# An issue order written out for the first 14 steps of an attention and FFN kernel

## Chip, core and metric

The kernel runs on one core of a Trainium2 chip. The metric is the device time of one execution in microseconds; lower is better. TensorE (PE) multiplies, VectorE (DVE) and ScalarE (ACT) work on tiles, GpSimd (POOL) helps, and SyncE (SP) issues the DMAs.

## What is computed

Attention of two kinds is added per head, and an FFN with a squared ReLU follows. All inputs are float32 (q, k, v and `w_in` eight times as large as drawn); the weights arrive as 8-byte words and are split in the kernel.

```python
B, H, S, D = q.shape                      # 8, 8, 576, 64; factor = 4, scale = 1/8
q_d, k_d, v_d = means over 4 neighbouring positions        # 144 positions
out_up = repeat(softmax(scale * q_d @ k_d.T) @ v_d, 4)
mask = abs(pos[:, None] - pos[None, :]) < 4
out_local = softmax(where(mask, scale * q @ k.T, -1e9)) @ v
x = (out_up + out_local)  ->  4608 tokens x 512
h = maximum(x @ w_in, 0)                  # 512 x 2048
out = (s * h * h + b) @ w_out             # 2048 x 512
```

## The kernel before

**FFN.** The tokens are cut into 18 blocks `t` of 256, the 2048 hidden columns into 8 pairs `p` of 256. A step (t, p) is `gemm1` (24 matmuls into one bank `ph`: high part times high, high times low, low times high), then on ScalarE ReLU, square and the rounding to `gh`, on VectorE the rest `gl`, then `gemm2` (12 matmuls into the two banks of `po` that collect block t). `gemm2` stands two or three steps behind. The order of steps is (0,0), (1,0), (0,1), (1,1) and so on to (1,6): steps 0 to 13; then block 2 with pairs 0 to 6: steps 14 to 20; then pair 7 of blocks 0 to 2; then blocks 3 to 17.

**Weights.** Pair p of `w_in` and `w_out` is loaded as 64-bit words into a stage buffer (`load_w`, `wst`) and split by `convert` into a float32 value `f`, its rounded part `hi` and the rest `lo`: one ScalarE multiply, four VectorE instructions on `es`, one ScalarE cast, one VectorE subtraction. A conversion here means one such run over 512 columns; a pair of weights has four. Pair 7 comes in eight quarters through buffers `pv` (`load_quarter`). `add_rows` adds up the rows of `w_out` on VectorE into `bias`, 31 additions of 512 columns, and `column_sums` makes b times their sum of it, used by the outputs.

**Attention.** A batch has four pairs of heads. For batches 0 to 2 `first_unit` does a pair: `down` (q and k summed by four into `qd` and `kd`, scores `sa`, exponentials `pd`, transposes `tp` and `tr`, product `up`) and the banded part (scores `sl`, `pl`, transpose, block matrix `db`, product `ol`), added into `x`. The pairs of batch 0 have rooms of their own in the buffers of later weights (`make_room`, zeroed by `clear`). `split_x` makes `xh` and `xl` from x for a block of tokens. A block needs all four pairs of its batch; block 2 needs batches 0 and 1.

**What sets the order.** The program is written as a sequence, and a scheduler lays out each engine's instructions by priorities and its own costs; each engine then runs its own list in order. Batch 0 has a high priority (offset 400), the conversions other ones (`BEHIND`), batch 1 is spread over the first steps (`advance`, `target`). A tile's bank in PSUM is fixed by its tag (`bank(i, ...)`).

Of the kernel before, what the change touches and what calls it, by code (L numbers as in the profile page):

```python
# [56 lines left out]
W_MAX = (1.875 - 2.0 ** -23) * 2.0 ** (31 - 127)  # L57

# [4 lines left out]
def attention_ffn_kernel(ctx, tc, qk, vw_in, vr_in, vdm, qkn, vn, w_in, w_out, s_in, b_in, out):  # L63
# [40 lines left out]
    def load_pair(b, hp):  # L104
        if (b, hp) in ld:
            return
        own = {}
        if b == 0 and hp:
            room[hp] = make_room(hp)
            own = room[hp]["load"]  # L110

        def load(tag, shape, src, pool=one):
            t = own[tag] if tag in own else pool.tile(shape, F32, tag=tag, name="t" + tag)
            nc.sync.dma_start(t, src)
            return t

        tqk = load("qk", [P, 2, SP], qk[b, hp], two)
        tvr = load("vr", [P, FAC, D], vr_in[b, hp])
        tvd = load("vd", [KM, FAC, P], vdm[b, hp])
        tvw = load("vw", [P, NG, P], vw_in[HP * b + hp]) if HP * b + hp < EU else None  # L120
        ld[(b, hp)] = (tqk, tvw, tvr, tvd)

    load_pair(0, 0)
# [4 lines left out]
    load_pair(0, 1)  # L128
# [43 lines left out]
    nc.vector.memset(db, 0.0)  # L174
# [7 lines left out]

    def clear(i):
# [30 lines left out]
    def convert(st, hi, lo, op, p):  # L214


        n = hi.shape[1]
        top, low = st[:, :, 1], st[:, :, 0]
        if p in (0, 1, 7):
            f = two.tile([P, n], F32, tag="pv", name="es")  # L220
        else:
            f = one.tile([P, n], F32, tag="xl2" if op == "i" else "os", name="es")
        w = f.bitcast(I32)


        nc.scalar.mul(f, top.bitcast(F32), 2.0 ** -112)
        nc.vector.tensor_scalar(f, f, W_MAX, -W_MAX, ALU.min, ALU.max)
        nc.vector.tensor_scalar(w, w, 3, 0x7FFFFFF8, ALU.logical_shift_left, ALU.bitwise_and)
        nc.vector.scalar_tensor_tensor(w, low, 29, w, ALU.logical_shift_right, ALU.bitwise_or)
        nc.vector.scalar_tensor_tensor(w, top, -0x80000000, w, ALU.bitwise_and, ALU.bitwise_or)  # L230
        nc.scalar.copy(hi, f)
        for i in range(0, n, 512):
            js = slice(i, min(i + 512, n))
            nc.vector.tensor_tensor(lo[:, js], f[:, js], hi.bitcast(F32)[:, js], ALU.subtract)

    def split_w(p):
        with tc.high_priority(offset=-BEHIND.get(p, 0)):
            split_parts(p)

    def split_parts(p):  # L240
        wi[p] = one.tile([P, 2, NK, 256], F32R, tag=f"wi{p}", name="wi")
        wo[p] = one.tile([P, 2, 2, DM], F32R, tag=f"wo{p}", name="wo")
        for op, w in (("i", wi[p]), ("o", wo[p])):
            fl = w.rearrange("p s k f -> p s (k f)")
            if p < len(STAGE):
                st = wst.pop((p, op))
                for j in range(0, 1024, CHUNK[p]):
                    js = slice(j, j + CHUNK[p])
                    convert(st[:, js], fl[:, 0, js], fl[:, 1, js], op, p)
            else:  # L250
                for i in range(4):
                    cs = slice(256 * i, 256 * i + 256)
                    convert(load_quarter(p, op, i), fl[:, 0, cs], fl[:, 1, cs], op, p)
# [14 lines left out]
    def down(b, hp, banks, tmp, dg):  # L268

        _, qc, vdr, vm = dg  # L270
        tqk, _, tvr, tvd = ld[(b, hp)]
        qt, kt = tqk[:, 0], tqk[:, 1]

        qd = tmp([P, SD], "qd")
        kd = tmp([P, SD], "kd")
        nc.vector.tensor_reduce(
            qd, qt[:, 0:S].rearrange("p (s j) -> p s j", j=FAC), AX.X, ALU.add)
        nc.vector.tensor_reduce(
            kd, kt[:, 3 : 3 + S].rearrange("p (s j) -> p s j", j=FAC), AX.X, ALU.add)
        for h in range(2):  # L280
            hs = slice(64 * h, 64 * h + 64)
            nc.scalar.copy(
                qc[hs, :, GQ * h : GQ * h + GQ], qd[hs].rearrange("p (i s) -> p i s", i=NQ))
# [17 lines left out]
        with first(b):  # L301
            for i in range(NQ):
                nc.tensor.matmul(sa[:, i], qc[:, i], kd, start=True, stop=True)  # L303
        nc.vector.tensor_reduce(dmx[:, 0], sa, AX.X, ALU.max, negate=True)
        nc.scalar.mul(dmx[:, 1], dmx[:, 0], SCALE / 16)
# [38 lines left out]
    def first_unit(b, hp, banks):  # L344
# [20 lines left out]
        tqk, vw, _, _ = ld[(b, hp)]  # L365
# [3 lines left out]
        dn = down(b, hp, banks, tmp, dg)  # L369
        next(dn)  # L370
        yield
        next(dn)
        yield

        own = room[hp] if b == 0 and hp else None
        pl = own["pl"] if own else two.tile([P, 2 * NG, 32], F32, tag="pl", name="pl")
        sm = own["sm"] if own else two.tile([P, 2, 2 * NG], F32, tag="sm", name="sm")
        lmx, lsm = sm[:, 0], sm[:, 1]  # L380
        for h in range(2):
            sl = banks([P, NG, 32], "sl")
            nc.tensor.matmul(sl, idb, maskb, start=True, stop=False)
            hs = slice(64 * h, 64 * h + 64)
            for g in range(NG):
                for w in range(4):
                    c0 = TW * (4 * g + w)
                    nc.tensor.matmul(
                        sl[32 * w : 32 * w + 32, g, :],
                        qt[hs, c0 : c0 + 32], kt[hs, c0 : c0 + 32],  # L390
                        start=False, stop=g == NG - 1, tile_position=(64 * h, 32 * w))
            hg = slice(h * NG, h * NG + NG)
            nc.vector.tensor_reduce(lmx[:, hg], sl, AX.X, ALU.max)
            nc.vector.tensor_tensor(
                pl[:, hg], sl, lmx[:, hg].unsqueeze(2).to_broadcast([P, NG, 32]), ALU.subtract)
            yield
        nc.scalar.activation(pl, pl, AF.Exp, scale=SCALE)
        nc.vector.tensor_reduce(lsm, pl, AX.X, ALU.add)
        nc.vector.tensor_scalar(lsm, lsm, 1e-9, None, ALU.add)
        nc.vector.reciprocal(lsm, lsm)  # L400
        (nc.vector if b else nc.gpsimd).tensor_tensor(
            pl, pl, lsm.unsqueeze(2).to_broadcast([P, 2 * NG, 32]), ALU.mult)
        yield
        next(dn)
        yield
        next(dn)
        if own:
            pt = take(sc, spots["vt"], [P, 2 * NG, 32])
        else:
            pt = two.tile([P, 2 * NG, 32], F32, tag="pl", name="pt")  # L410
        nc.vector.transpose(pt, pl)
        for w in range(4):
            ws = slice(32 * w, 32 * w + 32)
            nc.scalar.copy(bd[ws, :, ws], pt[ws])
        yield
# [4 lines left out]
        ups = tmp([P, SD], "ups")  # L420
        nc.scalar.copy(ups, up)
        yield
        for f in range(2):
            n = S // 2 // FAC
            ol = banks([P, S // 2], "ol")
            for gg in range(NG // 2):
                g = f * (NG // 2) + gg
                for h in range(2):
                    hs = slice(64 * h, 64 * h + 64)
                    pw = bd[:, h * NG + g, :].rearrange("p (w c) -> p w c", w=4)  # L430
                    nc.tensor.matmul(  # L431
                        ol[hs, 96 * gg : 96 * gg + 96], vw[:, g, hs], pw[:, :, 0:TW],
                        start=True, stop=True)
            nc.vector.tensor_tensor(
                x[:, hp, f * (S // 2) : (f + 1) * (S // 2)].rearrange("p (s j) -> p s j", j=FAC),
                ol.rearrange("p (s j) -> p s j", j=FAC),
# [333 lines left out]
```

## Time and profile before

| | |
|---|---|
| time of the runs | 970.22 us median of 3 (969.37 to 974.18) |
| span of the profiled execution | 970.7 us (its own time is not told apart from the runs) |
| TensorE busy | 938.7 us, 97% |
| VectorE, ScalarE, GpSimd busy | 637.7, 475.0, 418.0 us |
| granted TensorE clock, mean | 1.000 |
| moved by DMA | 86.26 MB |

Busy time counts an instruction from start to end, and instructions of one engine overlap a little. An engine's idle time is what its busy time leaves of a stretch. In the tables of windows each engine has its busy microseconds and its count of instructions; in the timeline a row gives start, length, engine, line, instruction and, in brackets, the idle time just before it and what ended that.

### The profile page before, as it was taken

Reading aid. Unit: us, or ns where it says so; the run is one execution under the profiler, and the core shown is the slowest. Engines: PE = TensorE matmul, PEld = TensorE weight load, DVE = VectorE, ACT = ScalarE, POOL = GpSimd, SP = SyncE. Lnnn points to the kernel's source line nnn. Section 1 sums busy time; section 2 is a strip of 40 time slices with the busy share of each in tenths; the row PEclk is TensorE's granted clock in tenths of the full one; section 3 lists DMA queues with packets and bytes.
Section 4 is the critical chain, followed back from the end, with each engine's and each line's share of the span. In section 5 each row is a group of like instructions: output and inputs, shape, how many; then the busy total and the mean of one; then the engine's idle time right before and its main releaser. Section 6 shows DMA issues by size and latency. Waiting matters only on the chain.

```text
span 970.7 us, 18541 instructions
## 1 busy us (share of the span) xinstructions
PE 938.7 (97%) x7316; PEld 843.4 (87%) x7316; DVE 637.7 (66%) x1175; ACT 475.0 (49%) x1141; POOL 418.0 (43%) x455
## 2 busy tenths in 40 slices
PE   5769999999999999999999999999999999999998
PEld 4559988888999999998888899989899999998987
DVE  5999996864567878787787878787878521211121
ACT  5878775553754453545363545453635433333231
POOL 9421011101066686776868786867676200000000
PEclk9999999999999999999999999999999999999999
DMA  9736512112243232323241424242412000000000
GB/s 316 261 121 210 172 60 78 49 42 73 101 134 113 77 110 72 102 70 133 67 136 66 135 68 131 72 134 69 136 55 76 1 22 1 23 1 22 1 23 22
DMA packets 32103, 86.26 MB, mean 89 GB/s; under 512 B 3344, under 2 KB 7952, under 8 KB 32016
## 3 DMA queue, kind: packets, MB, share of 16 engines
q1 hardware_dynamic: 32016, 85.08, 26.6%
q8 instruction: 57, 0.93, 0.4%
q14 instruction: 30, 0.25, 0.1%
HBM read 75.63 MB, written 9.44 MB: 88 GB/s over the span
## 4 chain that ended last, share of the span: by engine, by line
PE 74%; DVE 9%; DMA 8%; POOL 5%; ACT 2%; issue 2%; SPq 0%; DVEq 0%; ACTq 0%; POOLq 0%
PE ph L556 11%; PE ph L557 11%; PE ph L558 11%; PE po L603 11%; PE po L601 11%; PE po L602 11%; DMA tqk<-in_qk_dram 3%; POOL pr L466 3%; POOL acc L488 3%; DMA wst<-in_moe_w_out_dram 2%; PE sa L303 2%; DVE bias L579 1%; PE up L339 1%; PE ol L431 1%; DMA lqk<-in_qkn_dram 1%
## 5 line engine op out<-in xcount | busy, mean ns | idle before, releaser
L556 PE MATMUL ph<-xh,wi 128*128 128x256 f32 x1152 | 325.4, 283 | 3.7 <-ACT xh L542 2.5
L557 PE MATMUL ph<-xl,wi 128*128 128x256 f32 x1152 | 323.9, 281 | 0.0
L558 PE MATMUL ph<-xh,wi 128*128 128x256 f32 x1152 | 323.6, 281 | 0.0
L466 POOL TENSOR_TENSOR pr<-lqk 128x576 f32<-128x576 f32 x140 | 201.2, 1461 | 73.2 <-DMA lqk<-in_qkn_dram 29.2
L556 PEld LDWEIGHTS ph<-xh,wi 128*128 128x128 f32 x1152 | 217.5, 189 | 11.2 <-ACT xh L542 2.8
L557 PEld LDWEIGHTS ph<-xl,wi 128*128 128x128 f32 x1152 | 217.4, 189 | 5.4 <-issue 0.2
L558 PEld LDWEIGHTS ph<-xh,wi 128*128 128x128 f32 x1152 | 217.6, 189 | 0.3
L566 ACT ACTIVATE ph<-ph 128x512 f32<-128x512 f32 x144 | 83.8, 582 | 229.0 <-PE ph L558 223.2
L601 PE MATMUL po<-wo,gh 128*128 128x512 f32 x456 | 180.7, 396 | 0.0
L602 PE MATMUL po<-wo,gh 128*128 128x512 f32 x456 | 180.5, 396 | 0.0
L603 PE MATMUL po<-wo,gl 128*128 128x512 f32 x456 | 177.9, 397 | 0.0
L569 DVE TENSOR_TENSOR gl<-ph,gh 128x512 fp32r<-128x512 f32 x114 | 77.8, 683 | 115.8 <-ACT gh L568 115.5
L488 POOL TENSOR_TENSOR acc<-acc,pv 128x576 f32<-128x576 f32 x80 | 114.4, 1430 | 57.1 <-DVE acc L488 29.5
L468 DVE TENSOR_REDUCE st<-pr 128x9 f32<-128x576 f32 x140 | 105.9, 757 | 37.7 <-POOL pr L466 35.4
L292 POOL TENSOR_TENSOR dq<-vq 64x64 f32<-64x64 f32 x58 | 22.8, 393 | 197.4 <-PE up L337 195.3
L603 PEld LDWEIGHTS po<-wo,gl 128*128 128x128 f32 x456 | 85.7, 188 | 17.6 <-issue 0.2
L487 DVE TENSOR_TENSOR pv<-lv,st 128x576 f32<-128x576 f32 x120 | 87.5, 747 | 18.8 <-POOL acc L488 18.4
L601 PEld LDWEIGHTS po<-wo,gh 128*128 128x128 f32 x456 | 85.7, 188 | 15.9 <-ACT gh L568 0.6
L602 PEld LDWEIGHTS po<-wo,gh 128*128 128x128 f32 x456 | 85.7, 188 | 15.8
L568 ACT CAST gh<-ph 128x512 fp32r<-128x512 f32 x114 | 66.9, 587 | 64.3 <-PE po L602 62.4
L567 ACT ACTIVATE ph<-ph 128x512 f32<-128x512 f32 x144 | 83.7, 582 | 3.2
L602 PE MATMUL po<-wo,gb 128*128 128x512 f32 x120 | 47.1, 392 | 0.0
(149 smaller groups left out, 1239.3 us busy)
## 6 DMA issues: line engine op xcount, KB each, us to landing
tqk<-in_qk_dram SPq DMA_DIRECT2D x30, 584.0 KB, 4.1
lqk<-in_qkn_dram SPq DMA_DIRECT2D x20, 768.0 KB, 4.2
lv<-in_vn_dram SPq DMA_DIRECT2D x20, 480.0 KB, 3.4
out_dram<-os SPq DMA_DIRECT2D x17, 512.0 KB, 3.1
wst<-in_moe_w_in_dram SPq DMA_DIRECT2D x7, 1024.0 KB, 6.5
wst<-in_moe_w_out_dram SPq DMA_DIRECT2D x7, 1024.0 KB, 5.3
tvd<-in_vdm_dram SPq DMA_DIRECT2D x29, 160.0 KB, 2.9
tvr<-in_vr_dram SPq DMA_DIRECT2D x29, 128.0 KB, 3.1
```

Of the source, the lines that this page charges most:

```text
L466: nc.gpsimd.tensor_tensor(pr, lqk[:, 0:CH], lqk[:, CH + o : 2 * CH + o], ALU.mult)
L468: nc.vector.tensor_reduce(ls[:, :, o], pr, AX.X, ALU.add)
L487: nc.vector.tensor_tensor(pv, lv[:, o : o + CH], w, ALU.mult)
L488: (nc.vector if o % 3 == 1 else nc.gpsimd).tensor_tensor(acc[:, :, h], acc[:, :, h], pv, ALU.add)
L556: nc.tensor.matmul(ph[:, j], wi[p][:, 0, k, f], xh[:, k], start=(k == 0), stop=False)
L557: nc.tensor.matmul(ph[:, j], wi[p][:, 0, k, f], xl[:, k], start=False, stop=False)
L558: nc.tensor.matmul(ph[:, j], wi[p][:, 1, k, f], xh[:, k], start=False, stop=(k == NK - 1))
L566: nc.scalar.activation(ph, ph, AF.Relu)
L567: nc.scalar.activation(ph, ph, AF.Square)
L601: nc.tensor.matmul(po[m], gh[:, j, ms], wo[p][:, 0, j], start=first, stop=False)
L602: nc.tensor.matmul(po[m], gh[:, j, ms], wo[p][:, 1, j], start=False, stop=False)
L603: nc.tensor.matmul(po[m], gl[:, j, ms], wo[p][:, 0, j], start=False, stop=last)
```

## The change

The steps of batches 0 and 1, of the conversions of pairs 0 to 6 and of the first FFN steps become generators that stop after each piece of work on one engine (`banded` in place of `first_unit`'s body, `products1`, `upper`, `lower`, `products2`, `begin_x`, `third_x`). A string `PLAN` of 447 words names whose turn it is: `d0` to `d7` are the `down` parts of the eight pairs, `l0` to `l7` the banded parts, `v` the sums of values, `c0` to `c27` the conversions, `x` and `y` the splitting of x, `G`, `R`, `V`, `H` a half of the first product, the ScalarE part, `gl` and a half of the second product. `in_order` chains the instructions of each of four engines in the order in which they were issued, so the scheduler keeps that order among them; others may still go between. After the plan the old loop goes on from step 14.

Besides: the query blocks of batch 0 are loaded first; `clear` writes zeros on ScalarE and VectorE in place of GpSimd; the first two weight pairs are staged in different buffers; every `f` lies in `pv` (before, four tags were used); batch 1's chains each have one PSUM bank; the offsets' mask is made later; `add_rows` begins with pair 0 in place of 7, and is called from step 14 on; pair 7 is converted from step 14 on (before, step 11).

```diff
-STAGE = (6, 6, 7, 6, 7, 6, 7)
-CONVERT_AT = (1, 2, 4, 6, 7, 8, 11)
-CHUNK = (512, 512, 512, 1024, 1024, 512, 1024)
-BEHIND = {1: 400, 2: 100, 4: 100, 5: 400}
+STAGE = (7, 6, 7, 6, 7, 6, 7)
+CHUNK = 512
+PLAN = (
+    "d0 l0 d0 d1 d0 l0 d1 d2 l1 d0 l0 d2 d3 d0 v0 d1 l0 d0 d3 d0 l0 d2 d1 d0 l1 d1 d2 l1 l0 "
...
     def clear(i):
-        for j in range(0, n + QV, 488):
-            nc.gpsimd.memset(da[:, j : min(j + 488, n + QV)], 0.0)
-        nc.gpsimd.memset(vm, 0.0)
+        for part in (da[:, n : n + QV], vm, da[:, 0:n]):
+            if i == 3:
+                nc.vector.memset(part, 0.0)
+            else:
+                nc.scalar.copy(part, zero.to_broadcast([P, part.shape[1]]))
...
-        if p in (0, 1, 7):
-            f = two.tile([P, n], F32, tag="pv", name="es")
-        else:
-            f = one.tile([P, n], F32, tag="xl2" if op == "i" else "os", name="es")
+        f = two.tile([P, n], F32, tag="pv", name="es")
...
     def add_rows(p):
-        if p == NFP - 1:
+        if p == 0:
             nc.vector.tensor_tensor(bias, parts.pop(), parts.pop(), ALU.add)
...
+    @contextlib.contextmanager
+    def in_order():
+        traced = nc.cur_bb.bb.instructions
+        last = traced[-1]
+        yield
+        start = next(k for k in reversed(range(len(traced))) if traced[k] is last) + 1
+        for i in traced[start:]:
+            if i.engine in ENGINES:
+                if i.engine in tail:
+                    tc.add_manual_dep(i, tail[i.engine].name, ...)
+                tail[i.engine] = i
...
+    at = {"sa": 5, "tp": 5, "up": 5, "tr": 6, "sl0": 6, "sl1": 5, "ol": 6}
+    bk = {0: banks(*range(8)), 1: lambda shape, name: bank(at[name], shape, name)}
...
+    with tc.high_priority(offset=400):
+        with in_order():
+            for name in plan:
+                next(streams[name], None)
...
+    begin = 2 * HF
+    for st in range(begin, len(order)):
...
+        if st == begin:
+            split_w(NFP - 1)
+        if st - begin < NFP:
+            add_rows(st - begin)
```

What this does to the order of instructions is seen best on two engines. First VectorE at the start of the FFN, before: `es` are the steps of conversions, `xl` the rest of x, `x<-ol` the attention's sum of a pair.

```order
L543 TENSOR_TENSOR xl<-x,xh 128x1024
L227 TENSOR_SCALAR es<-es 128x512
L434 TENSOR_TENSOR x<-ol,ups 128x288
L234 TENSOR_TENSOR wi<-es,wi 128x512
L434 TENSOR_TENSOR x<-ol,ups 128x288
L234 TENSOR_TENSOR wo<-es,wo 128x512
L228 TENSOR_SCALAR es<-es 128x512
L227 TENSOR_SCALAR es<-es 128x512
L229 SCALAR_TENSOR_TENSOR es<-wst,es 128x512
```

The same place after, around the first `gl`, L642; L248 to L252 are the four steps on `es`.

```order
L251 SCALAR_TENSOR_TENSOR es<-wst,es 128x512
L252 SCALAR_TENSOR_TENSOR es<-wst,es 128x512
L642 TENSOR_TENSOR gl<-ph,gh 128x512
L248 TENSOR_SCALAR es<-es 128x512
L658 TENSOR_TENSOR bias<-bias,wo 128x512
L249 TENSOR_SCALAR es<-es 128x512
L251 SCALAR_TENSOR_TENSOR es<-wst,es 128x512
L252 SCALAR_TENSOR_TENSOR es<-wst,es 128x512
L258 TENSOR_TENSOR wo<-es,wo 128x512
L658 TENSOR_TENSOR bias<-bias,wo 128x512
```

Additions to `bias`, which before begin after `gl` of step 14, now stand among the first steps, and steps that read each other's result stand next to each other.

Then TensorE at the end of batch 0, before: `sl`, `tp`, `up` of batch 1's first pair stand ahead of the first matmul of the FFN, L556.

```order
L383 MATMUL sl<-maskb,idb 128x192
L388 MATMUL sl<-tqk 32x32 x24
L337 MATMUL up<-flat 128x144
L339 MATMUL up<-flat 128x144 x2
L322 MATMUL tp<-ident,pd 80x96
L325 MATMUL tp<-ident,pd 80x96 x2
L327 MATMUL tr<-ident,pd 64x96 x3
L337 MATMUL up<-ptr,dq 128x144
L339 MATMUL up<-ptm,dq 128x144 x2
L431 MATMUL ol<-flat 64x96 x12
L556 MATMUL ph<-xh,wi 128x256
```

After, with the FFN's matmuls at L622:

```order
L469 MATMUL ol<-flat 64x96 x12
L373 MATMUL up<-flat 128x144
L375 MATMUL up<-flat 128x144 x2
L469 MATMUL ol<-flat 64x96 x12
L426 LDWEIGHTS idb
L426 MATMUL sl_813<-maskb,idb 128x192
L431 MATMUL sl_813<-tqk 32x32 x24
L622 MATMUL ph<-xh,wi 128x256
```

Of batch 1 only one block of scores is left ahead of the FFN; the rest of its first pair comes after it.

More of the change, by code (lines that the diff above doesn't have):

```diff
@@ L102, in make_room, with load_parts, load_pair @@
                 "sm": take(pl, at + 384, [P, 2, 2 * NG])}
[L104 to L108, printed above, removed]
-            room[hp] = make_room(hp)
-            own = room[hp]["load"]
-        def load(tag, shape, src, pool=one):
+    def load_parts(b, hp, parts):
+        if b == 0 and hp and hp not in room:
+            room[hp] = make_room(hp)
+        own = room[hp]["load"] if b == 0 and hp else {}
+        got = ld.setdefault((b, hp), {})
+        for tag in parts:
+            shape, src, pool = {
+                "qk": ([P, 2, SP], qk[b, hp], two),
+                "vr": ([P, FAC, D], vr_in[b, hp], one),
+                "vd": ([KM, FAC, P], vdm[b, hp], one),
+                "vw": ([P, NG, P], vw_in[min(HP * b + hp, EU - 1)], one)}[tag]
             t = own[tag] if tag in own else pool.tile(shape, F32, tag=tag, name="t" + tag)
             nc.sync.dma_start(t, src)
[L115 to L123, printed above, removed]
+            got[tag] = t
+    def load_pair(b, hp):
+        if (b, hp) not in ld:
+            load_parts(b, hp, ("qk", "vr", "vd") + (("vw",) if HP * b + hp < EU else ()))
+    for hp in range(HP):
+        load_parts(0, hp, ("qk",))
+    for hp in range(HP):
+        load_parts(0, hp, ("vr", "vd"))
+    load_parts(0, 0, ("vw",))
     ident = cst.tile([P, P], F32, name="ident")
     make_identity(nc, ident)
-    load_pair(0, 1)
     mask = cst.tile([P, 3, 32], F32, name="mask")
@@ L236, in split_w @@
     def split_w(p):
-        with tc.high_priority(offset=-BEHIND.get(p, 0)):
-            split_parts(p)
+        for chunk in split_parts(p):
+            for _ in chunk:
+                pass
     def split_parts(p):
@@ L266, in first, with add_values @@
         return tc.high_priority() if b >= 3 else contextlib.nullcontext()
[L268 to L283, printed above, removed]
+    def add_values(b, hp, tmp, dg):
+        _, _, vdr, vm = dg
+        tvr, tvd = ld[(b, hp)]["vr"], ld[(b, hp)]["vd"]
         vt = tmp([P, 2, P], "vt")
@@ L292, in down @@
             ve.tensor_tensor(vdr[hs, hs], vq[hs, 0], vq[hs, 1], ALU.add)
+    def down(b, hp, banks, tmp, dg):
+        _, qc, vdr, vm = dg
+        tqk = ld[(b, hp)]["qk"]
+        qt, kt = tqk[:, 0], tqk[:, 1]
+        qd = tmp([P, SD], "qd")
+        kd = tmp([P, SD], "kd")
+        nc.vector.tensor_reduce(
+            qd, qt[:, 0:S].rearrange("p (s j) -> p s j", j=FAC), AX.X, ALU.add)
+        nc.vector.tensor_reduce(
+            kd, kt[:, 3 : 3 + S].rearrange("p (s j) -> p s j", j=FAC), AX.X, ALU.add)
+        yield
+        for h in range(2):
+            hs = slice(64 * h, 64 * h + 64)
+            nc.scalar.copy(
+                qc[hs, :, GQ * h : GQ * h + GQ], qd[hs].rearrange("p (i s) -> p i s", i=NQ))
         yield
@@ L370, in first_unit, with down_unit @@
+        return {"d": far(), "v": values(), "l": near()}
+    def first_unit(b, hp, banks):
+        part = banded(b, hp, banks)
+        for steps in ("ddv", "ddd", "ll", "ll", "lll", "ddd", "ddll", "dd", "ll", "ll"):
+            for which in steps:
+                next(part[which])
+            yield
+    def down_unit(b, hp, banks):
+        x = new_x(b)
+        tmp = lambda shape, name: one.tile(shape, F32, tag=name, name=name)
+        dn = down(b, hp, banks, tmp, diag[0])
         next(dn)
+        next(dn)
+        add_values(b, hp, tmp, diag[0])
@@ L371, in first_unit @@
         yield
[L372 to L395, printed above, removed]
-            yield
@@ L397, in first_unit @@
[L397 to L415, printed above, removed]
+        for count in (3, 3, 2):
+            for _ in range(count):
+                next(dn)
+            yield
         try:
@@ L419, in first_unit @@
             up = e.value
[L420 to L436, printed above, removed]
-                ups[:, n * f : n * f + n].unsqueeze(2).to_broadcast([P, n, FAC]), ALU.add)
-            if f == 1:
-                complete.add((b, hp))
-            yield
-    def down_unit(b, hp, banks):
-        x = new_x(b)
-        up = yield from down(
-            b, hp, banks, lambda shape, name: one.tile(shape, F32, tag=name, name=name),
-            diag[0])
         nc.scalar.copy(
@@ L586, in gemm2, with products2 @@
     def gemm2(t, p):
+        for _ in products2(t, p):
+            pass
+    def products2(t, p):
         if (t, p) == (0, NFP - 1):
@@ L610, in gemm2 @@
                     nc.sync.dma_start(out[r0 : r0 + P, cs], os_[:, m, cs])
-        if p == NFP - 1 and not end:
-            for m in range(2):
-                nc.vector.scalar_tensor_tensor(
-                    os_[:, m], po[m], sb_s, bias, ALU.mult, ALU.add)
-            nc.sync.dma_start(
-                out[TB * t : TB * t + TB, :].rearrange("(m p) c -> p m c", p=P), os_)
+            elif p == NFP - 1 and m == 1:
+                for i in range(2):
+                    nc.vector.scalar_tensor_tensor(
+                        os_[:, i], po[i], sb_s, bias, ALU.mult, ALU.add)
+                nc.sync.dma_start(
+                    out[TB * t : TB * t + TB, :].rearrange("(m p) c -> p m c", p=P), os_)
+            yield
     units = [(b, hp) for b in range(B) for hp in range(HP)]
@@ L636, in attention_ffn_kernel, with all_chunks, until @@
     nc.sync.dma_start(sb_b, bass.AP(b_in.tensor, b_in.offset, [[0, P], [1, 1]]))
-    clear(1)
-    bk = banks(0, 1, 2, 3, 5, 6, 7)
-    for hp in range(HP):
-        load_ahead(hp)
-        if hp > 1:
-            clear(hp)
-        with tc.high_priority(offset=400):
-            for _ in first_unit(0, hp, bk):
-                pass
-    split_w(0)
-    load_w(1)
-    load_w(2)
-    split_x(0)
-    split_x(1)
-    order = [(t, p) for p in range(HF) for t in range(2)]
-    order += [(2, p) for p in range(HF)]
-    order += [(t, p) for p in range(HF, NFP) for t in range(3)]
-    order += [(t, p) for t in range(3, NB) for p in range(NFP)]
+    load_w(1)
+    load_pair(1, 0)
+    load_pair(1, 1)
+    with tc.high_priority(offset=400):
+        with in_order():
+            nc.vector.memset(dq, 0.0)
+            for hp in range(1, HP):
+                clear(hp)
+            nc.vector.memset(db, 0.0)
+    offset_mask()
+    at = {"sa": 5, "tp": 5, "up": 5, "tr": 6, "sl0": 6, "sl1": 5, "ol": 6}
+    bk = {0: banks(*range(8)), 1: lambda shape, name: bank(at[name], shape, name)}
+    def all_chunks():
+        for p in range(HF):
+            if p > 1:
+                load_w(p)
+            if 1 < p < 4:
+                load_pair(1, p)
+            yield from split_parts(p)
+    streams = dict((f"c{i}", chunk) for i, chunk in enumerate(all_chunks()))
+    for b, hp in units[: 2 * HP]:
+        for name, steps in banded(b, hp, bk[b]).items():
+            streams[f"{name}{HP * b + hp}"] = steps
+    streams["x"] = begin_x()
+    streams["y"] = third_x()
+    streams["G"] = (None for t, p in order for _ in products1(t, p))
+    streams["R"] = (upper(t, p) for t, p in order)
+    streams["V"] = (lower(t, p) for t, p in order)
+    streams["H"] = (None for t, p in order for _ in products2(t, p))
+    plan = PLAN.split()
+    with tc.high_priority(offset=400):
+        with in_order():
+            for name in plan:
+                next(streams[name], None)
+    gone = {kind: plan.count(kind) for kind in "GRVH"}
+    def until(kind, count):
+        while gone[kind] < count:
+            next(streams[kind])
+            gone[kind] += 1
     need = [0, 2 * HF - 3] + [(S * b // TB) * NFP - 3 for b in range(2, B)]
@@ L664, in attention_rest @@
     def attention_rest():
-        for i in range(HP, EU):
+        for i in range(2 * HP, EU):
             load_ahead(i)
@@ L705, in attention_ffn_kernel @@
             split_x(splits[t, p])
-    for tp in pend:
-        gemm2(*tp)
+    until("H", 2 * len(order))
 def _layout(q, k, v):
```

205 lines of the change are left out of this document (164 added, 41 removed), and 15 rows, old and new, of the table PLAN.

## The prediction

> **What bounds the kernel now.** I read the page's slices first, then windows of the start, then the timeline of the engine to which they point.
>
> ```profile
> PE   5769999999999999999999999999999999999998
> DVE  5999996864567878787787878787878521211121
> ```
>
> TensorE has gaps in the first three of forty slices (73 us) and is full from then on. VectorE is full in slices two to six.
>
> ```profile
> core 0: us, PE busy (x) PEld busy (x) DVE busy (x) ACT busy (x) POOL busy (x), PEclk, DMA share, GB/s
> 0.00:25.00 25.00, 14.16 (x281) 11.22 (x281) 13.01 (x29) 12.15 (x39) 22.68 (x64) 1.00 0.96 315
> 75.00:125.00 50.00, 50.00 (x526) 45.05 (x527) 48.27 (x88) 40.10 (x86) 6.46 (x11) 1.00 0.51 171
> 30.00:40.00 10.00, 9.48 (x184) 7.46 (x174) 10.00 (x25) 9.38 (x27) 3.59 (x5) 1.00 0.93 312
> 0.00:64.57 64.57, 42.08 (x677) 33.99 (x677) 51.35 (x119) 44.07 (x128) 37.78 (x81) 1.00 0.74 247
> 0.00:161.30 161.30, 136.89 (x1614) 118.86 (x1615) 139.27 (x283) 116.05 (x279) 48.45 (x99) 1.00 0.54 181
> 73.70:158.00 84.30, 84.30 (x872) 75.31 (x871) 76.23 (x143) 63.54 (x138) 10.66 (x18) 1.00 0.42 139
> 158.00:210.80 52.80, 51.22 (x508) 43.85 (x507) 41.46 (x82) 25.23 (x65) 4.47 (x6) 1.00 0.17 52
> ```
>
> To the first FFN matmul TensorE worked 42.08 us and idled 22.5. VectorE worked 139.27 of the first 161.30 us: 22.0 idle, 12.0 of it in the first 25.
>
> ```profile
> 7.28 1.72 PE L303 MATMUL sa<-kd,dq 128*96 128x144 f32 x6 [7.28 <-DVE kd L278]
> 59.88 2.19 PE L431 MATMUL ol<-flat 128*64 128x96 f32 x24 [0.27 <-ACT flat L414]
> 64.57 0.58 PE L556 MATMUL ph<-xh,wi 128*128 128x256 f32 x1 [2.50 <-ACT xh L542]
> 100.23 1.21 PE L431 MATMUL ol<-db,tvw 128*64 128x96 f32 x24
> ```
>
> The first FFN matmul starts at 64.57. The same 24 matmuls of `ol` took 2.19 us just before it and 1.21 later: batch 0's attention runs at about half pace, though the clock column reads 1.00.
>
> **The unit of account.** The change lays down steps 0 to 13 and batch 1, so I compare the moment when VectorE ends `gl` of step 13. Now that is 161.3:
>
> ```profile
> 160.61 0.69 DVE L569 TENSOR_TENSOR gl<-ph,gh 128x512 fp32r<-128x512 f32 x1
> ```
>
> **VectorE's sum.** Durations overlap, so I take start to next start where it doesn't wait:
>
> ```profile
> 34.17 0.59 DVE L304 TENSOR_REDUCE flat<-sa 96x3 f32<-96x432 f32 x1
> 34.69 0.41 DVE L228 TENSOR_SCALAR es<-es 128x512 int32<-128x512 int32 x1
> 35.02 0.34 DVE L393 TENSOR_REDUCE flat<-sl 128x6 f32<-128x192 f32 x1
> 35.29 0.67 DVE L229 SCALAR_TENSOR_TENSOR es<-wst,es 128x512 int32<-128x512 int32 x1
> 35.89 0.34 DVE L394 TENSOR_TENSOR flat<-sl,flat 128x192 f32<-128x192 f32 x1
> 36.16 0.73 DVE L276 TENSOR_REDUCE qd<-tqk 128x144 f32<-128x576 f32 x1
> 36.82 0.73 DVE L278 TENSOR_REDUCE kd<-tqk 128x144 f32<-128x576 f32 x1
> 37.48 0.41 DVE L227 TENSOR_SCALAR es<-es 128x512 f32<-128x512 f32 x1
> 37.81 0.68 DVE L230 SCALAR_TENSOR_TENSOR es<-wst,es 128x512 int32<-128x512 int32 x1
> 38.41 0.54 DVE L398 TENSOR_REDUCE flat<-flat 128x12 f32<-128x384 f32 x1
> 38.88 0.41 DVE L228 TENSOR_SCALAR es<-es 128x512 int32<-128x512 int32 x1
> ...
> 43.65 0.58 DVE L411 STREAM_TRANSPOSE flat<-flat 128x384 f32<-128x384 f32 x1 [0.20 <-POOL flat L401]
> 44.15 0.38 DVE L228 TENSOR_SCALAR es<-es 128x512 int32<-128x512 int32 x1
> 44.46 0.45 DVE L434 TENSOR_TENSOR x<-ol,flat 128x288 f32<-128x288 f32 x1
> 44.83 0.68 DVE L234 TENSOR_TENSOR wo<-es,wo 128x512 fp32r<-128x512 f32 x1
> 45.42 0.35 DVE L394 TENSOR_TENSOR flat<-sl,flat 128x192 f32<-128x192 f32 x1
> ...
> 97.09 1.23 DVE L229 SCALAR_TENSOR_TENSOR es<-wst,es 128x1024 int32<-128x1024 int32 x1
> 98.35 1.22 DVE L230 SCALAR_TENSOR_TENSOR es<-wst,es 128x1024 int32<-128x1024 int32 x1
> ...
> 105.59 1.21 DVE L230 SCALAR_TENSOR_TENSOR es<-wst,es 128x1024 int32<-128x1024 int32 x1
> 106.72 0.42 DVE L228 TENSOR_SCALAR es<-es 128x512 int32<-128x512 int32 x1
> ...
> 177.56 0.68 DVE L569 TENSOR_TENSOR gl<-ph,gh 128x512 fp32r<-128x512 f32 x1
> 178.16 0.68 DVE L579 TENSOR_TENSOR bias<-bias,wo 128x512 f32<-128x512 f32 x1
> ```
>
> A 512-column conversion is 0.33 + 0.33 + 0.60 + 0.60 + 0.59 = 2.46 us. A pair of batch 0 is qd and kd 1.32, four score steps of 0.27, dmx 0.52, row sum 0.47, transpose 0.50, two additions of 0.37 and 0.3 of small ones: 4.9. A pair of batch 1 multiplies on VectorE too: 5.4. A `gl` takes 0.60; so does a bias addition, of the same size. Ahead of step 13's `gl` the new order holds: 28 conversions 68.9; batch 0, 19.7; batch 1, 21.6; 14 `gl`, 8.4; 26 bias additions, 15.6; six pieces of `xl`, 3.6; the start of batch 2, 3.2; memsets and casts 4.2 (estimate, sized by columns). Sum 145.2.
>
> To this comes a cost of neighbours. Where an instruction reads what the one just ahead of it wrote, the first takes 1.26 (97.09 to 98.35); where not, 1.13 (105.59 to 106.72): 0.13 more. The order of now has 29 such neighbours to this point, since pieces of several chains alternate; the new one has 92, as a plan's step issues its two or three instructions together. 92 x 0.13 = 12.0, so 157.2 us of VectorE against 139.3 now: the bias additions, which now stand behind step 14, and the neighbours outweigh the five quarters of pair 7 that now lie ahead.
>
> **VectorE's idle time after.** (1) 0.9 until its first instruction (estimate: the same as now). (2) Batch 0: by the 42.08 row TensorE did five pairs less one `ol`, so (42.08 + 2.19) / 5 = 8.85 a pair, 35.4 for four. From 7.3 as now, with a score block of the next pair and waits (3 us, estimate: a third of a pair) the last `ol` is out at 45.7. Ahead of the addition that reads it VectorE holds 39 us of work and 27 neighbours (3.5): it idles 45.7 - 42.5 - 0.9 = 2.3, say 2. Bounds: 0 (TensorE at full pace) and 12 (the first 25 us of now). The first FFN matmul comes near 48. (3) For the 115 us from there 75 to 125 us is the nearest row: 1.73 of 50 idle, 3.5%. I take 2.5%, 2.9 us, because bias additions that wait for nothing recent stand between; bounds 1 and 12. `gl` of step 13 then ends at 157.2 + 0.9 + 2 + 2.9 = 163.0: 1.7 us later than now, although the FFN starts 16 us earlier.
>
> TensorE is not the limit. Steps 0 to 13 took it 84.3 us, fully busy, with most of batch 1's first pair done before; a whole pair at full pace is 4.4 (half of 8.85). From 48 + 6 for the first step it would need 88, until 142. Full now in this stretch, it will wait some 20 us there, for VectorE.
>
> **After step 13.** In the new order TensorE has 12 second-product matmuls of step 12 behind it at that `gl`, a half step more than now: 1.4 us ahead (estimate: six of 0.23, a quarter of a step's 5.5). From 158 to 210.8 it now idles 1.58, most of it here, where 31 bias additions crowd VectorE; five are left there after:
>
> ```profile
> 177.10 0.26 PE L383 MATMUL sl<-maskb,idb 128*128 128x192 bf16 x1 [1.06 <-DVE pl L394]
> ```
>
> I count 1.6 won, and 1.0 for batch 2's pairs, which find VectorE free. Sum: -1.7 + 1.4 + 1.6 + 1.0 = 2.3 us won: 970.7 - 2.3 = 968.4 of span. The profiled span stands 0.5 above the runs' median (970.22), so the time is 968: no change that can be told.
>
> **The other edits.** GpSimd loses block memsets; ScalarE takes two sets of them, 4416 columns, VectorE one. At 0.59 per 512 columns (the nearest row) ScalarE's end near 7 us, when the first query block is ready: between 0 and 2 us late, taken as 0, with the query load as cover. Banks of batch 1: each wait costs 0 to 1.06 (the row above) and TensorE has 20 us to spare: 0. Conversions have two temporaries (`pv`) in place of four: 0 while VectorE is the bound, else rival 2. SyncE: query blocks move ahead of value loads; the second stage's weights have a buffer of their own; batch 1's value loads stand ahead of the third stage in a queue that issues in order, and wait for GpSimd, which has time after 25 us. 0, covered by the second stage's conversions (9.8 us).
>
> **The pace of early attention.** In 30 to 40 us TensorE was 95% busy and at 59.88 still slow; only dense FFN matmuls changed that. The Trainium skill, TensorE: Matmul & The Clock Gate, Part 1, has the clock double after some 3.4 us of sustained activity, small matmuls or not. By that rule term 2 would fall to 0 and the time to 966. The row speaks against it here.
>
> **Rivals.** (1) Faster: the bias additions fall into waits. In the new order several stand right ahead of a step that waits for ScalarE. If half of them cost nothing, 7.8 us more are won: 960. For it: ScalarE is part of each conversion. Against: VectorE idles only 3.5% now in this stretch, so there are few waits.
>
> (2) Slower: the fixed order costs idle time. A conversion goes ScalarE, VectorE, ScalarE, VectorE through two temporaries, and a late piece holds all behind it. At 10% in term 3 (11.5 us) `gl` of step 13 ends 8.6 later: 977. It decides from 9%. For it: nothing on VectorE may pass. Against: ScalarE is 75% busy now.
>
> (3) Slower: pair 7's weights. They pass in eight quarters through `pv`, each load behind the quarter before:
>
> ```profile
> 149.35 2.75 DMA wst<-in_moe_w_in_dram
> ...
> 171.16 2.63 DMA wst<-in_moe_w_out_dram
> ```
>
> Four periods in 21.8 us: 5.45 each. All eight now come behind the last conversion, near 160, and stand on VectorE between `gl` of steps 14 to 19. A step takes 52.8 / 7 = 7.5 us there; above 7.5 a quarter it decides, since `gl` waits behind each. At 9 it loses 8 x 1.5 = 12 us: 980. At 5.45 it ends at 204, ahead of its use near 225.
>
> **Chances.** Forecast 0.50 (964 to 972), rival 1 0.25, rival 2 0.16, rival 3 0.09. A measurement tells 0.5% (4.85 us) from no change: faster 0.25 and 0.05 of the forecast's edge, same 0.45, slower 0.25. The range 958 to 977 leaves out rival 3 and the tails of 1 and 2; the likeliest case's own is 964 to 972.
>
> **What would show it.** First FFN matmul near 48, `ol` x24 near 2.2 until there; VectorE over 95% busy from 50 to 160; `gl` of step 13 near 163 with most bias additions ahead of it; TensorE with 15 us or more of waits for VectorE or ScalarE between 55 and 160. I am wrong if TensorE stays full there (then VectorE was not the bound), or if VectorE idles over 8%.

## The result, and the profile after

The changed kernel takes 980.93 us (median of 4 runs, 980.26 to 981.21), the kernel before 972.20 us beside it (969.37 to 975.57). The ratio is 1.0084, 95% interval 1.0056 to 1.0113: slower by 0.84%, where 968 was forecast. The profiled execution has a span of 979.0 us, against 970.7.

The page's slices of the changed kernel:

```profile
PE   5789789999999999999999999999999999999998
DVE  8999999563558787778787978787978621211111
```

TensorE's gaps, which ended with the third slice before, now reach into the sixth (147 us). VectorE is full in slices two to seven. Windows of the changed kernel (columns as in the prediction):

```profile
0.00:25.00 25.00, 13.99 (x380) 12.12 (x381) 20.49 (x47) 20.03 (x59) 14.92 (x42) 0.93 0.95 327
25.00:50.00 25.00, 19.21 (x241) 15.55 (x239) 22.73 (x48) 20.14 (x53) 11.24 (x19) 0.64 0.71 234
50.00:170.24 120.24, 104.61 (x1051) 89.40 (x1052) 114.45 (x227) 81.51 (x190) 12.93 (x24) 0.93 0.36 116
0.00:170.24 170.24, 137.81 (x1669) 117.07 (x1670) 157.68 (x319) 121.68 (x300) 39.10 (x84) 0.89 0.50 164
55.10:165.80 110.70, 96.38 (x963) 82.35 (x964) 104.98 (x207) 76.09 (x175) 12.93 (x24) 0.95 0.37 122
```

VectorE works 157.68 of the first 170.24 us and idles 12.6: 4.5 in the first 25 us, 2.3 in the next 25, 5.8 after. From step 0's Relu to step 13's (the last row) TensorE idles 14.3 of 110.7 us; before it idled nothing between these two. Its timeline, and VectorE's at step 13:

```profile
46.92 0.38 PE L622 MATMUL ph<-xh,wi 128*128 128x256 f32 x1
...
163.89 0.68 DVE L642 TENSOR_TENSOR gl<-ph,gh 128x512 fp32r<-128x512 f32 x1
164.49 0.68 DVE L658 TENSOR_TENSOR bias<-bias,wo 128x512 f32<-128x512 f32 x1
165.09 0.68 DVE L258 TENSOR_TENSOR wo<-es,wo 128x512 fp32r<-128x512 f32 x1
165.69 0.60 DVE L336 TENSOR_REDUCE dmx<-sa 96x3 f32<-96x432 f32 x1
166.21 0.74 DVE L317 TENSOR_REDUCE kd<-tqk 128x144 f32<-128x576 f32 x1
166.87 0.68 DVE L658 TENSOR_TENSOR bias<-bias,wo 128x512 f32<-128x512 f32 x1
167.47 0.45 DVE L473 TENSOR_TENSOR x<-ol,ups 128x288 f32<-128x288 f32 x1
167.84 0.95 DVE L754 TENSOR_TENSOR xl<-x,os 128x768 fp32r<-128x768 f32 x1
168.70 0.28 DVE L248 TENSOR_SCALAR es<-es 128x256 f32<-128x256 f32 x1
168.90 0.68 DVE L658 TENSOR_TENSOR bias<-bias,wo 128x512 f32<-128x512 f32 x1
169.50 0.68 DVE L642 TENSOR_TENSOR gl<-ph,gh 128x512 fp32r<-128x512 f32 x1
```

The first FFN matmul comes at 46.9 us, 17.7 earlier. `gl` of step 13 (the last row) ends at 170.2, 8.9 later than before, and between the `gl` of steps 12 and 13 no gap is left: VectorE works back to back, three bias additions among it, though nothing needs the bias before the first output, long after. The lead of 17.7 us is spent in 13 steps.

### The profile page after: what moved, and what is told of

The parts are those of the page before. It is cut to its first block, busy times and chain, and to the rows that moved or that the text cites. A ratio compares the mean times of both kernels' runs of the same rounds, so it can differ in the third digit from the quotient of the medians.

```text
span 979.0 us, 18567 instructions
## 1 busy us (share of the span) xinstructions
PE 937.8 (96%) x7316; PEld 842.0 (86%) x7316; DVE 647.3 (66%) x1204; ACT 481.4 (49%) x1161; POOL 405.9 (41%) x440
## 4 chain that ended last, share of the span: by engine, by line
PE 70%; DVE 16%; POOL 4%; DMA 3%; ACT 3%; issue 2%; DVEq 0%; POOLq 0%; SPq 0%; ACTq 0%
PE ph L622 32%; PE po L684 11%; PE po L685 11%; PE po L686 10%; DVE es L251 2%; POOL pr L527 2%; DVE bias L658 2%; DMA tqk<-in_qk_dram 2%; PE sa L334 2%; POOL acc L549 1%; DVE es L252 1%; DVE gl L642 1%; PE up L375 1%; DVE pv L548 1%; PE ot L559 1%
## 5 line engine op out<-in xcount | busy, mean ns | idle before, releaser
L622 PE MATMUL ph<-xh,wi 128*128 128x256 f32 x2176 | 411.7, 283 | 5.0 <-DVE gl L642 2.0
L622 PEld LDWEIGHTS ph<-xh,wi 128*128 128x128 f32 x2176 | 343.8, 190 | 12.5 <-DVE gl L642 2.8
L622 PE MATMUL ph<-xl,wi 128*128 128x256 f32 x1152 | 324.6, 282 | 1.3 <-DVE xl L744 1.3
L622 PEld LDWEIGHTS ph<-xl,wi 128*128 128x128 f32 x1152 | 218.0, 189 | 6.1 <-DVE xl L744 1.6
L635 ACT ACTIVATE ph<-ph 128x512 f32<-128x512 f32 x144 | 83.7, 582 | 222.9 <-PE ph L622 209.9
L642 DVE TENSOR_TENSOR gl<-ph,gh 128x512 fp32r<-128x512 f32 x114 | 78.0, 684 | 122.8 <-ACT gh L637 122.6
L684 PEld LDWEIGHTS po<-wo,gh 128*128 128x128 f32 x456 | 86.5, 190 | 20.3 <-ACT gh L637 4.8
L685 PEld LDWEIGHTS po<-wo,gh 128*128 128x128 f32 x456 | 86.6, 190 | 14.9
L548 DVE TENSOR_TENSOR pv<-lv,st 128x576 f32<-128x576 f32 x120 | 87.6, 748 | 15.8 <-POOL acc L549 15.3
L304 POOL TENSOR_TENSOR dq<-vt 80x64 f32<-80x64 f32 x58 | 19.0, 339 | 105.6 <-PE up L375 103.8
L685 PE MATMUL po<-wo,gb 128*128 128x512 f32 x120 | 46.9, 390 | 0.0
L686 PE MATMUL po<-wo,gb 128*128 128x512 f32 x120 | 46.8, 390 | 0.0
```

The costliest lines, as they stand in the source:

```text
L548: nc.vector.tensor_tensor(pv, lv[:, o : o + CH], w, ALU.mult)
L622: nc.tensor.matmul(ph[:, j], wi[p][:, s, k, f], xk[:, k], start=k == 0 and s == 0 and xk is xh, stop=k == NK - 1 and s == 1)
L635: nc.scalar.activation(ph, ph, AF.Relu)
L642: nc.vector.tensor_tensor(gl, acc.pop((t, p)), gh.bitcast(F32), ALU.subtract)
L684: nc.tensor.matmul(po[m], gh[:, j, ms], wo[p][:, 0, j], start=first, stop=False)
L685: nc.tensor.matmul(po[m], gh[:, j, ms], wo[p][:, 1, j], start=False, stop=False)
```

## Experiments

All are timed against the kernel before on the same chip; "step 13" is the end of its `gl`. The theory after the first comparison: VectorE sets the pace to step 13, and the bias additions, which the change lets the scheduler put there, cost their own length. The rivals were the written order's idle time, and a loss behind step 13.

**Late additions.** One edit on the changed kernel:

```
-            add_rows(st - begin)
+            with in_order() if st == begin else contextlib.nullcontext():
+                add_rows(st - begin)
```

> The changed kernel with one edit: the first bias addition is chained behind the last VectorE instruction of the written order, so that all 31 bias additions run after step 13. Theory (VectorE sets the pace of steps 0 to 13, and the 26 bias additions ahead of step 13 cost their 15.6 us there): `gl` of step 13 ends near 157 (170.2 with the change), and the kernel takes 966 to 972 us. Rival A (the written order itself makes VectorE wait, whatever else it carries): the additions leave idle time behind, step 13 stays near 168 and the time near 979. Rival B (what is won by step 13 is lost again after it, to pair 7's eight quarters and to the additions that now stand there): step 13 near 157 and the time still 977 to 981.

967.61 us (965.68 to 971.91); ratio 0.9962 (0.9946 to 0.9977). Step 13 ends at 157.8:

```profile
0.00:157.80 157.80, 134.74 (x1622) 115.40 (x1623) 144.19 (x293) 120.75 (x300) 37.68 (x84) 0.91 0.53 177
```

VectorE has 26 instructions fewer in the stretch and 13.5 us less work, and step 13 comes 12.4 us earlier; its idle time is 13.6 us, 1.0 more. So the additions found few waits to fall into: of the 16.2 us that 27 of them last (0.60 from start to start), 12.4 come off. Part of the rest is that neighbours which an addition had kept apart now follow each other. Behind step 13 they run from 158 to 213 us and nothing is lost there: the first products of step 24 end 77.8 us after step 13, in the changed kernel 78.2. Theory right in place and size; rivals A and B fall.

**Additions on GpSimd.** The edit is `nc.gpsimd` for `nc.vector` in `add_rows`.

> The changed kernel with the 31 bias additions on GpSimd in place of VectorE; GpSimd has next to nothing to do between 50 and 170 us. Theory (VectorE's work sets the pace): as in the run with late additions, `gl` of step 13 near 157, and since nothing has to be added later either, 964 to 970 us. Rival A (the order's idle time): near 979. Rival C (GpSimd's additions slow the VectorE instructions beside them): VectorE's conversions take longer each (L248 over 0.36 us, L251 over 0.64), step 13 at 163 or later, and a time above 973.

990.28 us (989.19 to 990.46); ratio 1.0187 (1.0173 to 1.0202); step 13 at 177.2. Rival C, and more than it asked for. (Its bounds of 0.36 and 0.64 us were set too low, being spacings: by busy time the changed kernel itself has 0.43 and 0.70.) The timeline of this run, with the rows of VectorE and GpSimd alone:

```profile
59.97 1.45 POOL L658 TENSOR_TENSOR bias<-bias,wo 128x512 f32<-128x512 f32 x1 [9.22 <-ACT wo L254]
60.31 1.66 DVE L251 SCALAR_TENSOR_TENSOR es<-wst,es 128x512 int32<-128x512 int32 x1
62.01 0.69 DVE L252 SCALAR_TENSOR_TENSOR es<-wst,es 128x512 int32<-128x512 int32 x1
62.62 1.46 DVE L258 TENSOR_TENSOR wo<-es,wo 128x512 fp32r<-128x512 f32 x2
...
63.50 4.55 POOL L658 TENSOR_TENSOR bias<-bias,wo 128x512 f32<-128x512 f32 x3 [2.08 <-ACT wo L254]
64.05 1.46 DVE L248 TENSOR_SCALAR es<-es 128x512 f32<-128x512 f32 x1
65.54 1.39 DVE L249 TENSOR_SCALAR es<-es 128x512 int32<-128x512 int32 x1
66.96 1.63 DVE L251 SCALAR_TENSOR_TENSOR es<-wst,es 128x512 int32<-128x512 int32 x1
68.63 0.69 DVE L252 SCALAR_TENSOR_TENSOR es<-wst,es 128x512 int32<-128x512 int32 x1
69.24 0.68 DVE L642 TENSOR_TENSOR gl<-ph,gh 128x512 fp32r<-128x512 f32 x1
```

Beside an addition of GpSimd a conversion instruction takes 1.4 to 1.7 us instead of 0.42 or 0.69: it lasts until GpSimd is done, and then runs. VectorE's work to step 13 is 163.4 us with 26 instructions fewer, more than the 157.7 with them:

```profile
0.00:177.20 177.20, 141.22 (x1629) 119.71 (x1630) 163.42 (x293) 121.08 (x300) 78.94 (x111) 0.88 0.48 158
```

Instructions with an operand in PSUM do not suffer, nor do the sums of q and k (L315, L317: 0.74 us beside an addition and alone). Of `gl` (L642) the five that overlapped an addition took 0.675 us on average, the nine others 0.683; of L251 the six that did took 1.51, the others 0.70. The Trainium skill, SBUF — State Buffer, "SBUF: two separate sides", has GpSimd and VectorE share one pair of ports as an exclusive lock for a whole instruction; the rows agree.

**No written order on one engine, or on any.** The edit takes VectorE, or all engines, out of `ENGINES`.

> The changed kernel with the written order laid on TensorE, ScalarE and GpSimd alone; VectorE's order is the scheduler's again. Rival A (the written VectorE order costs idle time): VectorE's 12.6 us of idle time up to step 13 shrink by some 6 us, step 13 ends near 164, time near 974. Theory (the work sets the pace, the order is near what the scheduler would find): step 13 within 3 us of 170 and 978 to 984 us.

986.71 us (983.51 to 989.13); ratio 1.0142 (1.0119 to 1.0165).

> The changed kernel with no written order on any engine: the same operations, tiles and banks, issued in the same sequence, but each engine's order is the scheduler's. Theory (what moved the time is the order, and what it puts ahead of step 13): the first FFN matmul comes later than 46.9 us, and the time is within 1 % of the kernel before on either side, 965 to 980. Rival D (the tiles and chunks that the change has made smaller, 512 columns in place of 1024, and the shared `pv` buffers cost the time, whatever the order): 980 us or more with VectorE's work to step 13 unchanged at 157 us.

975.20 us (972.95 to 978.83); ratio 1.0039 (1.0024 to 1.0054). The window to step 13 with VectorE free, and then with all engines free:

```profile
0.00:179.20 179.20, 144.26 (x1629) 123.12 (x1630) 155.56 (x317) 121.15 (x300) 40.42 (x84) 0.91 0.46 156
```

```profile
0.00:168.00 168.00, 138.67 (x1753) 116.72 (x1754) 154.71 (x329) 125.01 (x312) 41.12 (x90) 0.93 0.51 174
```

With VectorE alone free, its idle time is 23.6 us, not 6: rival A is refuted from its own side, and so is my expectation that step 13 would stay within 3 us of 170. Most of it is for ScalarE (12.0 us, against 2.2 in the changed kernel, counting waits over 0.1 us); that the other engines' fixed orders no longer fit VectorE's is the likely reason, not shown. With all free the kernel beats the changed one by 5.7 us. The first FFN matmul does come later, as expected (48.5 us against 46.9), though the first step's products end 2.4 us earlier (52.7 against 55.1). Rival D fell, and the idle time is about the same (13.3). What differs is VectorE's work: 154.7 us with ten instructions more, one attention unit of batch 2 among them.

**Dependent neighbours pulled apart,** on the kernel with late additions: a conversion's pairs become two steps each, and the plan puts another step between, where it had one.

```
         nc.vector.tensor_scalar(f, f, W_MAX, -W_MAX, ALU.min, ALU.max)
+        yield
         nc.vector.tensor_scalar(w, w, 3, 0x7FFFFFF8, ...)
...
-    "... G R c6 G c7 V c6 c7 G ..."
+    "... c6 G R c6 G c7 V c6 c6 c7 c7 G ..."
```

> The kernel with late additions (967.61 us, `gl` of step 13 at 157.8 us), with one more edit: in the written order the dependent VectorE neighbours of a conversion (L248 with L249, L251 with L252) are pulled apart, so that 11 of the 56 such pairs are left instead of 56, with an independent instruction between the two. Theory (a dependent neighbour costs VectorE some 0.12 us, and VectorE sets the pace to step 13): 42 to 45 such pairs fewer, about 5 us; VectorE's busy time to step 13 falls from 144.2 to near 139, step 13 ends near 153 and the kernel takes 961 to 965 us. Rival E (the pair cost is hidden in VectorE's idle time, or returns as such, since TensorE and ScalarE set the pace by now): busy time falls but step 13 stays within 1.5 us of 157.8 and the time within 2 us of 967.6.

968.66 us (967.38 to 971.57); ratio 0.9974 (0.9962 to 0.9986): no gain.

```profile
0.00:159.20 159.20, 132.74 (x1622) 113.19 (x1623) 141.31 (x293) 120.91 (x300) 36.77 (x84) 0.92 0.53 176
```

The busy time falls by 2.9 us, not 5, and the idle time grows by 4.3 (13.6 to 17.9): step 13 is 1.4 us later. Busy time does not hold the whole price of a neighbour. Behind an instruction whose result the next one reads VectorE stands some 0.03 us, and that counts as idle time. Such pauses (under 0.1 us, counted in the trace) come to 3.8 us in the kernel with late additions and 2.6 here. With them 4.1 us of the neighbours' cost are gone, and the longer waits grow by 5.5 us (9.8 to 15.3), 3.1 of it for ScalarE. That a piece which is moved one place back makes ScalarE, and then VectorE, wait is the likely reason, not shown. Rival E, though for the second of its reasons.

**TensorE's order free,** on the kernel with late additions (TensorE taken out of `ENGINES`).

> The kernel with late additions, the written order laid on VectorE, ScalarE and GpSimd alone; TensorE's order is the scheduler's. In the changed kernel without any written order, one more attention unit of batch 2 stood ahead of step 13 than with it (864 `sl` products against 816), and steps 14 to 24 took 68.6 us instead of 75.3. Theory (the written TensorE order keeps batch 2's attention out of TensorE's waits): step 13 within 2 us of 157.8, a unit of batch 2 more ahead of it, and 961 to 965 us. Rival F (TensorE's order without the plan delays what VectorE and ScalarE wait for, as VectorE's free order did): step 13 at 161 or later and 970 us or more.

974.40 us (971.75 to 975.46); ratio 1.0033 (1.0021 to 1.0045). Step 13 at 165.8. A unit of batch 2 does come ahead (816 `sl` products at step 13 against 768), but VectorE idles 20.3 us: rival F. One engine free among ordered ones is again worse than all or none.

**No written order and late additions:** the chain of the first experiment, with no plan order on any engine.

```
-            if i.engine in ENGINES:
-                if i.engine in tail:
+            if i.engine == nc.vector.engine:
+                if i.engine in tail and behind:
...
-            add_rows(st - begin)
+            behind = st == begin
+            with in_order():
+                add_rows(st - begin)
+            behind = False
```

> No written order on any engine, and the 31 bias additions chained behind `gl` of step 13: the fourth corner of a square with the changed kernel (written order, early additions: 980.9 us), late additions (967.6) and no written order (975.2). Theory (the additions cost VectorE's time ahead of step 13 whatever the order is): about as much falls as with the written order, 13 us: 961 to 965 us, step 13 near 155. Rival G (the scheduler had put the additions into VectorE's idle time, so that without the written order they cost little): 972 to 976 us, step 13 within 3 us of 168.

962.15 us (958.46 to 964.94); ratio 0.9910 (0.9889 to 0.9930): faster than the kernel before by 0.9% and, by the ratios, than the changed one by 1.7%. The theory held and rival G fell. The square is closed:

| | additions early | additions late |
|---|---|---|
| written order | 980.9 (1.0084) | 967.6 (0.9962) |
| no written order | 975.2 (1.0039) | 962.2 (0.9910) |

The additions cost 13.3 and 13.0 us, the written order 5.7 and 5.4. By the ratios, each against the kernel before beside it, it is 11.9 and 12.5, and 4.4 and 5.1; each of these is known to some 3 us. That one depends on the other is not seen. What else the change holds (earlier loads, a bank per chain, equal chunks, the new order of issue) is worth about 9 us to the good: 962.2 against 971.2. It was not taken apart.

Where the order's 5.4 us lie is seen in the two kernels with late additions, which have the same number of VectorE instructions ahead of step 13:

```profile
0.00:153.00 153.00, 132.05 (x1665) 112.55 (x1666) 138.03 (x293) 120.13 (x303) 37.78 (x84) 0.94 0.53 183
```

293 instructions take 138.0 us here and 144.2 with the written order; idle time is 15.0 against 13.6. The difference is in how instructions follow each other. Counted in the trace, 111 of the 293 start within 0.1 us after the end of the one ahead with the written order, 18 without; nearly all others start before that end, or after a longer wait. To the 6.2 us of busy time come the short pauses, 3.8 us with the order and 0.6 without: 9.4 us over 93 such neighbours, 0.10 each. Pulling apart gives the same price: 111 to 71, 4.1 us, 0.10. VectorE rows of the changed kernel, and then of the kernel without order and with late additions:

```profile
62.48 0.42 DVE L248 TENSOR_SCALAR es<-es 128x512 f32<-128x512 f32 x1
62.82 0.68 DVE L658 TENSOR_TENSOR bias<-bias,wo 128x512 f32<-128x512 f32 x1
...
66.28 0.42 DVE L248 TENSOR_SCALAR es<-es 128x512 f32<-128x512 f32 x1
66.74 0.43 DVE L249 TENSOR_SCALAR es<-es 128x512 int32<-128x512 int32 x1
```

```profile
60.22 0.42 DVE L248 TENSOR_SCALAR es<-es 128x512 f32<-128x512 f32 x1
60.55 0.42 DVE L249 TENSOR_SCALAR es<-es 128x512 int32<-128x512 int32 x1
60.89 0.22 DVE L446 RECIPROCAL sm<-sm 128x12 f32<-128x12 f32 x1
```

L248 holds VectorE 0.46 us where L249 needs its result, 0.34 where an addition follows; in the free order L248 and L249 of two different chunks alternate, 0.33 apart. The written order wins back about half of this: its longer waits come to 9.8 us, against 14.4 without order, and step 13 is 4.8 us later. That the neighbours are the order's cost is shown for VectorE's work (two runs, one price); for the kernel's time it is not, since pulling them apart won nothing and a piece of batch 2 also comes earlier in the free order.

## Why the prediction was wrong

The place was right, the sizes were not. Against the forecast span (968.4) the changed kernel's is 10.6 us longer. By the prediction's terms:

- **VectorE's work to step 13:** forecast 157.2, measured 157.7 by busy time. But the forecast counted from start to start, and so with the short pauses behind neighbours; there are 98 of these, 3.4 us, which the busy time leaves out. Counted like the forecast the work is 161.1: +3.9. The neighbours were sized about right: the rows of L248 above differ by 0.12, the two runs give 0.10, the forecast had 0.13. What was left out is VectorE beside GpSimd: eight instructions that overlap one of GpSimd's last 1.9 us longer than others of their kind (L252 at 30.0 us 1.10 in place of 0.69). Six more neighbours than forecast and a 27th addition make up some 1.3; the last 0.7 I did not find. The kernel before had such long instructions too (13, 3.8 us longer in all), so the place to see them was there.
- **Its idle time (terms 1, 2 and 3): term 2 failed.** Forecast 0.9 + 2 + 2.9 = 5.8; measured 12.56, less the 3.43 of short pauses 9.1: +3.3. From 50 us on the longer waits are 3.3 us, 2.8% of 120, where I took 2.5%: term 3 was right within 0.5 us. In the first 50 us they are 5.8, against 2.9. The one wait of term 2, for the last `ol` of batch 0, is not among them. In its place stand ten of 0.1 to 1.6 us: 0.9 at the start as forecast, and then 1.9 for GpSimd, 1.6 for TensorE's scores, 0.9 for ScalarE and 0.5 that the profile puts down to nothing. The four corners of the square idle 12.6 to 15.0 us to step 13; without the short pauses it is 9.1 and 9.8 with the written order, 12.8 and 14.4 without, so this is no cost of the fixed order (rival 2). With 161.1 and 9.1 in place of 157.2 and 5.8 the working would have said 975.
- **After step 13: the largest failure.** Forecast 4.0 us to the good (1.4 + 1.6 + 1.0). At the end of step 24's first products the changed kernel is 10.0 us behind (248.4 against 238.4), 1.1 more than at step 13: +5.1 against the forecast. Counting each matmul at the median spacing of its shape (an estimate from the trace), TensorE had 67.9 us of work there, 70.1 before: of the 2.4 us for second products and batch 2, 2.2 are there. But the time it lost there did not fall by 1.6 us; it grew by 3.3 (10.3 against 7.0). Some 4 of the 10.3 us (an estimate: the wait and the slower matmuls behind it) are one place, shown in the changed kernel's timeline:

```profile
180.91 0.44 ACT L246 ACTIVATE es<-wst 128x256 f32<-128x256 f32 x1 [2.97 <-DMA wst<-in_moe_w_in_dram]
...
181.25 0.59 ACT L635 ACTIVATE ph<-ph 128x512 f32<-128x512 f32 x1
...
182.58 2.05 ACT L459 COPY db<-pt 32x384 f32<-32x384 f32 x4
...
184.65 0.59 ACT L637 CAST gh<-ph 128x512 fp32r<-128x512 f32 x1
...
185.28 0.60 PE L684 MATMUL po<-wo,gh 128*128 128x512 f32 x1 [2.43 <-ACT gh L637]
185.69 0.63 PE L685 MATMUL po<-wo,gh 128*128 128x512 f32 x1
```

ScalarE first waits 2.97 us for a load of pair 7, with this step's ReLU (L635) behind it: the step's products end at 180.48 and the ReLU starts at 181.25. Then it does four copies of an attention unit ahead of `gh`. TensorE waits 2.43 us for `gh`, and goes on at half pace: 0.42 us from one 512-column matmul to the next instead of 0.23, granted clock 0.83 from 180 to 190 us. I named what went away there (the crowd of additions) and not what is late next.

- **The rest:** from step 24 to the end the changed kernel is 1.7 us shorter (730.6 against 732.3), which nothing in the forecast spoke of. 3.9 + 3.3 + 5.1 - 1.7 = 10.6.

Of the signs named: the first FFN matmul came at 46.9 (48); VectorE is 95.2% busy from 50 us to step 13 (over 95%); 27 additions are ahead of step 13 (most). Wrong were step 13 (170.2 for 163) and, just, TensorE's idle time (14.3 for 15).

**Rival 1** (additions in waits, 960) is refuted: it asked for half of them to cost nothing, and they cost 12.4 of their 16.2 us. **Rival 2** (fixed order idles) was right that the order costs, 4.4 to 5.7 us, and wrong how: the longer waits are shorter with it. **Rival 3** (pair 7's quarters) did not decide: their eight loads start 6.8 us apart on average (160.4 to 207.8), under the 7.5 named. One of them has its part in the wait at 185 us.

**The pace of early attention** went against my argument, and in part with the Trainium skill, TensorE: Matmul & The Clock Gate, Part 1 (clock up after some 3.4 us of sustained activity, down after as long an idle window). From 15 us on, behind 3.41 us in which TensorE was busy throughout (11.46 to 14.87), the denser attention ran at full pace; then TensorE stood 3.63 us, and was at half pace from there:

```profile
18.05 0.62 PE L431 MATMUL sl<-flat 64*32 64x32 f32 x48
...
22.81 0.55 PE L431 MATMUL sl<-flat 64*32 64x32 f32 x24 [3.63 <-issue]
...
40.06 2.19 PE L469 MATMUL ol<-flat 128*64 128x96 f32 x24
...
43.72 1.21 PE L469 MATMUL ol<-flat 128*64 128x96 f32 x24 [0.54 <-ACT flat L459]
```

Up to here the trace agrees. But the half pace then lasted until 42 us, though TensorE was busy for 16.9 of these 20.5 us and throughout from 25.1 to 28.5; and at 185 us a wait of 2.43 us was enough to bring it back. So the 2 us that this rule would have taken off term 2 were not to be had.

## What to carry to other kernels

When a change pulls the critical work forward, ask what else its engine may now do first: 27 additions that nobody waits for cost some 12 us because they were ready early, and one dependency that holds them back won all of it. Count forecast and measurement alike: the short pauses behind neighbours stood in the forecast's work and in the measured idle time. Look for what GpSimd does beside VectorE, and price the next wait wherever a wait is taken away. An order written by hand has to count how VectorE's instructions follow each other. Freeing VectorE alone or TensorE alone cost 6 to 7 us more than leaving all engines ordered; the other two were not tried.

## What was not expected of the hardware

GpSimd is no free place for additions: one of 1.3 us beside VectorE's conversion instructions stops these until it ends, and 31 of them cost the kernel 9.4 us more than on VectorE (990.3 against 980.9).

TensorE's stop of 3.63 us at 19 us falls into the middle of a block of 48 matmuls whose other half had been issued, and waits for nothing that the profile shows. In the trace a transfer of 16 KB of instructions begins at 20.3 and takes 1.2 us, while data transfers keep the DMA engines 95% busy. In the kernel with late additions the stop is 3.35 us, from 20.05, and such a transfer begins at 21.1. But two more such transfers, at 14.0 and 26.8 us in the changed kernel, come without a stop. That TensorE waited for instructions is possible, and was not tested.

In the profile of before the clock column reads 1.00 while matmuls ran at half pace; in the changed kernel's it falls to 0.64 (25 to 50 us). The trace has its first record of the granted clock at 72.6 us before and at 14.9 in the changed kernel, each a rise to full, and the column reads 1.00 ahead of it as well. The spacing of equal matmuls tells the pace in both. Between 55 us and step 13 the changed kernel falls to half pace twice more (0.50 from 100.2 to 107.0 and from 124.2 to 127.5); the kernel with late additions does not.
